# Two interleaved attention layers on one Trainium2 core: what the recurrent layer does at the border between two segments is reordered

## The chip, the cores and the metric

The kernel runs on one core of one Trainium2 chip. A core has five engines with an instruction queue each: PE (TensorE, matrix products; PEld are its weight loads), DVE (VectorE), ACT (ScalarE), POOL (GpSimd) and SP (SyncE, which here only issues transfers). They work side by side and wait for each other through semaphores. Sixteen DMA engines move data. TensorE writes to PSUM, eight banks of 2 KB per partition; everything else on the chip lies in SBUF.

The metric is the device time of one execution in microseconds (us), the median of several runs. The profile is of one execution of its own.

## The reference

The input x (1 x 2048 x 640) goes through four layers, A B A B, each added to its input after a layer norm. Layer B is a linear attention over all rows. Layer A is a recurrent attention with a memory:

```python
for s in range(n_seg):                       # 64 segments of 32 rows
    h = concat([mem, x[32 * s:32 * s + 32]]) # 8 memory rows + 32 rows, 640 columns
    q, k, v = h @ Wq, h @ Wk, h @ Wv         # 32 heads of 192
    p = softmax(mask(q k^T * scale))         # memory rows see all; others are causal
    o = (p v) @ Wo
    mem = o[:8]                              # the memory of the next segment
    outs.append(o[8:])
```

So the 64 segments of a layer form a chain: the first eight rows of one segment's output are inputs of the next segment's three projections.

## The kernel before

Everything the change touches is in the method A_chain, the chain of 64 segments of one layer A. The instructions are in an order written out by hand: each engine runs its own in the order in which the code issues them, with no scheduler between. Where an operation needs a result, a free buffer or a PSUM bank from another engine, it waits, and everything behind it on its engine's queue waits too.

**Rounds.** A segment has four rounds (n = 0 to 3) of eight heads. A round has the projections Q, K and V (project, L996 in the profile: 20 products each, of the transposed rows hT with 384 columns of weights), the scores (L1033 adds the mask, L1038 the six products), the exponential E (weigh, L1110), the product with the values (attend, L1049 into ps_o; L1056 into ps_t), the reciprocal of the sums rc (L1063), the scaling of the outputs osc (L1069 on ACT, L1071 on DVE), the transposition of osc to OT (turn, L1174 and L1181), and the output product with that round's part of Wo (wo_round, L1093), which adds up over the rounds in one PSUM bank, W. The rounds are interleaved: while the scores of round n are weighed, Q and K of round n+1 are projected.

**Copies.** Projections come out of PSUM on ACT as raw (to_raw, L1006), and DVE transposes them into QT and KT (to_rows, L1011 to L1016). V is copied by ACT for one half (L1025) and DVE for the other (L1027) into one of two tiles Vp.

**Rows that need no memory.** Of each segment's 32 rows, 24 go through the chain with the 8 memory rows. Keys, queries and values of the last 8 rows, the tails, were computed for all segments beforehand; POOL fetches them (kqb L967, Vp<-vb L979) and copies them into QT and KT (L972 to L975). The outputs of the tails collect in ps_t over two rounds and are weighed, transposed and stored for a later output product (keep_tail: reciprocal rct L1075, otr L1077 on ACT, otb L1079 on DVE; store_tail: L1083 on POOL).

**Weights.** Part of Wq, Wk, Wv and Wo stays in SBUF, and part takes turns: when round 0 has used a piece, SP loads the piece for round 3 of the same segment into its place (L680); after the output product of round 0 the same for Wo (L696). SP issues in the order Q, K, V, Wo.

**The border.** When W is complete, four partial sums lie in four partition groups of it. DVE transposes them into wt (L1244) in two pieces of the columns, 96 and 64, and adds the two halves into the first eight columns of hT (L1247). The first projections of the next segment start with the parts of hT that come first. Then keep_rows makes the 24 finished rows: ACT copies half of W to wh (L955), DVE adds the other half (L958), first for one half of the columns and then for the other. keep_tail follows. store_rows (L963, POOL) writes the rows after the next segment's Q0 and K0. A product with nothing to compute (keep_busy, L1099) and a weight load (fill, L1105) stand on PE between the segments. Most of hT for the next segment is transposed before that from rows fetched earlier (hx_transpose, L946).

**PSUM.** The eight banks are: two for Q and K, two for scores, one each for V, ps_o, ps_t and W.

Of the kernel before, what the change touches and what calls it, by code (L numbers as in the profile page):

```python
# [8 lines left out]
P = 128  # L9
BF16 = mybir.dt.bfloat16  # L10
F32 = mybir.dt.float32
ACT = mybir.ActivationFunctionType
ALU = mybir.AluOpType
# [104 lines left out]
class Kernel:  # L118
# [800 lines left out]
    def A_chain(self, xn_dram, at_dram, li, load_slot, piece, load_wo, late_wo, wo_mid, wo_end, low):  # L919
# [3 lines left out]
        with tc.tile_pool(name=f"A{li}_ch", reuse_waits="tile", bufs=1) as sp, \  # L923
# [27 lines left out]

            def keep_rows(W):
                tmp = [sp.tile([P, 160], F32, name=f"wh{a}", tag=tag) for a, tag in enumerate(("E", "rawk"))]
                for a in range(2):
                    last = nc.scalar.activation(out=tmp[a][64:P, :], in_=W[64:P, 160 * a:160 * a + 160], func=ACT.Copy)  # L955
                    for g in range(2):
                        c = 320 * a + 160 * g
                        nc.vector.tensor_tensor(out=orow[:, c:c + 160], in0=W[32 * g:32 * g + 32, 160 * a:160 * a + 160],  # L958
                                                in1=tmp[a][64 + 32 * g:96 + 32 * g, :], op=ALU.add)
                self.chain_end = [last]  # L960
# [57 lines left out]
            def v_rows(pv, n, which="ax"):  # L1018
                for x in range(2):
                    if "ax"[x] not in which:  # L1020
                        continue
                    o = self.two_heads(Vs[n % 2][0:64, 2 * VH * x:2 * VH * x + 2 * VH])
                    i = pv[64 * x:64 * x + 64, 0:384].rearrange("p (e f) -> p e f", e=2)
                    if x == 0:
                        nc.scalar.activation(out=o, in_=i, func=ACT.Copy)  # L1025
                    else:
                        nc.vector.tensor_copy(out=o, in_=i)  # L1027

            def scores():

                S = pop.tile([P, 512], F32, name="ps_s", tag="s", bufs=2)
                m = self.mk[0:80, :]
                nc.tensor.matmul(S[0:80, 0:320], lhsT=self.ident[0:80, 0:80], rhs=ap3(m, [list(m.ap[0]), [0, 4], [1, 80]]),  # L1033
                                 start=True, stop=False, skip_group_check=True)
                for x in range(2):
                    for i, q0, q1 in ((0, 0, 1), (1, 1, 3), (2, 3, 4)):
                        c0 = 160 * x + (80 if i == 2 else 0)
                        nc.tensor.matmul(S[0:80, c0:c0 + 80 * (q1 - q0)], lhsT=KT[:, 3 * x + i, :], rhs=QT[:, x, q0:q1, :],  # L1038
                                         start=False, stop=(x == 1 and i == 2), skip_group_check=True)
                return S  # L1040
# [32 lines left out]
            def keep_tail(tag):  # L1073
                rc = sp.tile([P, 1], F32, name="rct", tag="rct")
                nc.vector.reciprocal(out=rc[:], in_=pair[0][:, 192:193])  # L1075
                rows = sp.tile([P, 192], BF16, name="otr", tag=tag)
                nc.scalar.activation(out=rows[:], in_=pair[0][:, 0:192], func=ACT.Copy, scale=rc[:])  # L1077
                otb = sp.tile([P, 192], BF16, name="otb", tag="otb")
                self.chain_end.append(nc.vector.transpose(out=otb[:], in_=rows[:]))  # L1079
                return otb  # L1080
# [55 lines left out]
            for s in range(NSEG):  # L1136
                W = pop.tile([P, 512], F32, name="ps_w", tag="w")
# [22 lines left out]
                to_rows(q_or_k("K", 0), "K")  # L1160
                if s == 0:
                    late_wo(2)
                if s > 0:
                    store_rows(s - 1)
                pv = v_banks()
                project(hT, pv, "V", 0, s, range(KC))
                v_rows(pv, 0)
                OTs = []

                def turn(n, osc):  # L1170
# [9 lines left out]
                    for G, v in enumerate(OTs[n]):  # L1180
                        nc.vector.transpose(out=v, in_=osc[:, 192 * G:192 * G + 192].rearrange("p (c j) -> p c j", j=64))  # L1181
# [3 lines left out]
                for n in range(L):  # L1185
# [7 lines left out]
                    elif n == 2:  # L1193
                        wo_round(W, order[1], OTs[1], False, False, range(6))
                        self.chain_end = []
                        otb = keep_tail("rawk")
# [16 lines left out]
                    v_rows(pv, n + 1)  # L1213
# [11 lines left out]
                osc = sp.tile([P, 384], BF16, name="osc", tag="raw")  # L1225
                scaled(osc[:, 0:192], O, rc, 0, "s")
                scaled(osc[:, 192:384], O, rc, 1, "v")
                turn(L, osc)
# [11 lines left out]
                if s + 1 < NSEG:  # L1240
                    wt = [sp.tile([P, KC, 32], F32, name=f"wt{a}", tag=tag) for a, tag in enumerate(("raw", "rawk"))]
                    for b0, b1 in ((2, 5), (0, 2)):
                        for a in range(2):
                            nc.vector.transpose(out=wt[a][:, b0:b1, :],  # L1244
                                                in_=W[:, 160 * a:160 * a + 160].rearrange("p (j b) -> p b j", b=KC)[:, b0:b1, :])
                        for a in range(2):
                            nc.vector.tensor_tensor(out=hT[64 * a:64 * a + 64, b0:b1, 0:8], in0=wt[a][0:64, b0:b1, 0:8],  # L1247
                                                    in1=wt[a][64:P, b0:b1, 0:8], op=ALU.add)
                keep_rows(W)
                store_tail(keep_tail("OTh"), s, order[L])  # L1250
# [85 lines left out]
```

## Time and profile before

| | |
|---|---|
| time, median of 3 runs | 3744.9 us (3744.84 to 3748.18) |
| profiled execution, its own time | 3738.74 us |
| its span, first to last instruction | 3737.0 us |
| mean granted TensorE clock | 0.979 |
| PE busy | 3223.9 us (86%) |
| DVE busy | 2628.7 us (70%) |
| ACT busy | 1753.6 us (47%) |
| POOL busy | 1446.6 us (39%) |
| DMA | 927.76 MB, mean 248 GB/s |

A row of a timeline gives start, length, engine, line, operation, what is written and read, shapes and count; in brackets stand the idle time of the engine before it and what ended that. A row of the list of waits gives who waited for whom, the total in us, how often, and the longest. A stretch of time gives its length, the busy time of each engine with the number of instructions, the granted clock as a share of the full one, the busy share of the DMA engines and GB/s. The share can pass 1.0, since packets overlap. The two layers A take most of the span: 64 segments each, of some 22 us.

### The profile page before, as it was taken

How to read it: one execution, taken by the hardware profiler on the slowest of the kernel's cores; microseconds unless marked ns; L12 is line 12 of the kernel's file. 1: busy time of each engine (PE TensorE's matmuls, PEld its weight loads, DVE VectorE, ACT ScalarE, POOL GpSimd, SP SyncE). 2: the span in 40 equal slices, each digit the busy share in tenths (PEclk: the TensorE clock that was granted, in tenths of full speed). 3: DMA queues.
4: the chain of work that ended last, by engine and by line, in shares of the span. 5: the costliest groups of instructions: out<-in, count | busy, mean ns of one | idle time of the engine just before them, and what ended most of it. 6: DMA issues, size and time to landing. Idle time of an engine off the chain costs nothing.

```text
span 3737.0 us, 143258 instructions
## 1 busy us (share of the span) xinstructions
PE 3223.9 (86%) x58528; PEld 1965.6 (53%) x58834; DVE 2628.7 (70%) x7607; ACT 1753.6 (47%) x4225; POOL 1446.6 (39%) x3917
## 2 busy tenths in 40 slices
PE   9878888888888888889999788888888888888899
PEld 7644555555554555555467455555555555555553
DVE  5467777777777777756643677777777777777575
ACT  3244444444444444446533445444444444445463
POOL 3344444444444444431122344444444444444310
PEclk9999999999999999999999999999999999999999
DMA  8887777777777777770375878777777777788600
GB/s 321 322 284 260 269 279 276 272 265 272 279 278 260 273 267 278 267 248 12 124 270 206 282 264 280 277 268 266 263 276 273 273 269 259 267 281 280 237 4 29
DMA packets 444876, 927.76 MB, mean 248 GB/s; under 512 B 71722, under 2 KB 203450, under 8 KB 441146
## 3 DMA queue, kind: packets, MB, share of 16 engines
q1 hardware_dynamic: 382746, 821.50, 61.9%
q0 software_dynamic: 59552, 83.85, 7.1%
q10 hardware_dynamic: 1920, 13.24, 0.9%
q8 instruction: 461, 7.55, 0.8%
q14 instruction: 197, 1.61, 0.1%
HBM read 850.47 MB, written 75.69 MB: 248 GB/s over the span
## 4 chain that ended last, share of the span: by engine, by line
PE 42%; DVE 25%; DMA 10%; ACT 9%; issue 9%; POOL 3%; PEld 2%; ACTq 0%; SPq 0%; POOLq 0%; DVEq 0%
PE ps_qk L996 11%; PE ps_w L1093 8%; DMA Vp<-vb 7%; ACT osc L1069 4%; PE ps_v L996 4%; PE ps_pre L878 3%; PE ps_s L1038 3%; DVE Vp L958 3%; ACT otr L1077 2%; DVE KT L1011 2%; DVE QT L1014 2%; DVE otb L1079 2%; ACT wh L955 2%; PE kv L1291 2%; DVE Vp L1027 2%
## 5 line engine op out<-in xcount | busy, mean ns | idle before, releaser
L996 PE MATMUL ps_qk<-arena,hT 128*32 128x384 bf16 x20480 | 1051.7, 336 | 175.7 <-DVE hT L1247 96.0
L996 PEld LDWEIGHTS <-hT 128*32 128x32 bf16 x30720 | 784.2, 98 | 603.4 <-DVE hT L1247 159.4
L1006 ACT ACTIVATE raw<-ps_qk 128x384 bf16<-128x384 f32 x1024 | 489.2, 490 | 326.2 <-PE ps_qk L996 291.2
L996 PE MATMUL ps_v<-arena,hT 128*32 128x384 bf16 x10240 | 515.6, 328 | 9.6 <-DMA arena<-in_A_Wv_dram 9.6
L1093 PE MATMUL ps_w<-arena,OT 128*32 128x320 bf16 x9216 | 452.0, 303 | 8.1 <-DMA arena<-wo_rows 5.1
L1069 ACT ACTIVATE osc<-ps_o,rc 128x192 bf16<-128x192 f32 x896 | 335.3, 418 | 214.8 <-DVE rc L1063 214.1
L972 POOL COPY QT<-kqb 128x64 bf16<-128x64 bf16 x512 | 120.1, 235 | 644.8 <-PE ps_s L1038 585.4
L967 POOL DMA_DIRECT2D kqb<-kqb x512 | 290.5, 568 | 165.3 <-POOL KT L975 147.1
L1083 POOL DMA_DIRECT2D otb<-otb x256 | 143.8, 562 | 533.8 <-DVE otb L1079 506.9
L1014 DVE STREAM_TRANSPOSE QT<-raw 128x256 bf16<-128x256 bf16 x512 | 222.5, 434 | 177.3 <-PE ps_s L1038 157.3
L1110 ACT ACTIVATE E<-ps_s 80x320 bf16<-80x320 f32 x512 | 220.4, 431 | 268.5 <-PE ps_s L1038 267.8
L1011 DVE STREAM_TRANSPOSE KT<-raw 128x384 bf16<-128x384 bf16 x512 | 296.1, 578 | 54.0 <-ACT raw L1006 45.1
L955 ACT ACTIVATE wh<-ps_w 64x160 f32<-64x160 f32 x256 | 76.6, 299 | 507.7 <-PE ps_qk L996 366.0
L1027 DVE CAST Vp<-ps_v 64x384 bf16<-64x384 f32 x512 | 286.0, 559 | 27.4 <-ACT Vp L1025 11.5
L1038 PE MATMUL ps_s<-QT,KT 128*80 128x80 bf16 (+1 forms) x3072 | 233.8, 213 | 81.7 <-DVE KT L1011 48.5
L1093 PEld LDWEIGHTS <-OT 128*32 128x32 bf16 x9216 | 221.5, 96 | 143.1 <-DVE OT L1174 66.5
L979 POOL DMA_DIRECT2D Vp<-vb x512 | 258.7, 505 | 24.6 <-PE ps_t L1056 9.7
L1038 PEld LDWEIGHTS <-KT 128*80 128x80 bf16 x3072 | 198.2, 119 | 126.7 <-issue 112.9
L1093 PE MATMUL ps_w<-arena,KT 128*32 128x320 bf16 x3072 | 133.9, 310 | 143.2 <-DVE KT L1181 142.6
L1025 ACT ACTIVATE Vp<-ps_v 64x384 bf16<-64x384 f32 x512 | 246.6, 482 | 19.6 <-PE ps_v L996 19.5
L1049 PE MATMUL ps_o<-Vp,E 80*32 80x193 bf16 x4096 | 187.8, 249 | 39.7 <-DMA Vp<-vb 34.1
L878 PEld LDWEIGHTS <-arena 128*128 128x128 bf16 x1920 | 190.0, 99 | 43.5 <-issue 12.0
(155 smaller groups left out, 5053.7 us busy)
## 6 DMA issues: line engine op xcount, KB each, us to landing
arena<-wo_rows SPq DMA_DIRECT2D x804, 320.0 KB, 6.9
arena<-in_A_Wq_dram SPq DMA_DIRECT2D x427, 384.0 KB, 4.4
arena<-in_A_Wv_dram SPq DMA_DIRECT2D x427, 384.0 KB, 6.2
arena<-in_A_Wk_dram SPq DMA_DIRECT2D x768, 192.0 KB, 5.7
kqb<-kqb POOLq DMA_DIRECT2D x512, 48.0 KB, 4.9
arena<-in_A_Wk_dram SPq DMA_DIRECT2D x43, 384.0 KB, 7.8
vb<-arena POOLq DMA_DIRECT2D x128, 97.0 KB, 6.2
Vp<-vb POOLq DMA_DIRECT2D x512, 24.2 KB, 4.8
```

The costliest lines, as they stand in the source:

```text
L878: nc.tensor.matmul(ps[:, T * i:T * i + T], lhsT=w[b][:, P * c:P * c + P], rhs=xBT[:, b, :], start=(b == 0), stop=(b == KC - 1))
L967: nc.gpsimd.dma_start(out=kqb[:], in_=self.kqb_d[r, :, s, :])
L979: nc.gpsimd.dma_start(out=Vs[n % 2][64:80, :], in_=self.vb_d[s, r].rearrange("g t f -> (g t) f"))
L996: nc.tensor.matmul(o[32 * g:32 * g + 32, 0:384], lhsT=hT[:, b, :], rhs=rhs, start=(i == 0), stop=(i == KC - 1), tile_position=(0, 32 * g), ...
L1006: nc.scalar.activation(out=raw[:], in_=ps[:, 0:384], func=ACT.Copy)
L1011: nc.vector.transpose(out=KT[:, :, 0:64], in_=raw[:, :].rearrange("p (c j) -> p c j", j=64))
L1014: nc.vector.transpose(out=QT[:, :, 0:4:3, 0:64], in_=rv[:, :, 0:3:2, :])
L1025: nc.scalar.activation(out=o, in_=i, func=ACT.Copy)
L1027: nc.vector.tensor_copy(out=o, in_=i)
L1038: nc.tensor.matmul(S[0:80, c0:c0 + 80 * (q1 - q0)], lhsT=KT[:, 3 * x + i, :], rhs=QT[:, x, q0:q1, :], start=False, stop=(x == 1 and i == 2 ...
L1069: nc.scalar.activation(out=out, in_=i, func=ACT.Copy, scale=rc[:, G:G + 1])
L1093: nc.tensor.matmul(W[q:q + 32, 0:320], lhsT=OT[i // 6][:, i % 6 // 2, 32 * (i % 2):32 * (i % 2) + 32], rhs=rhs, start=(first and i < 2), s ...
```

## The change

- **Finished rows.** keep_rows and store_rows leave the border. They run in round 0 of the next segment, after turn(0) and ahead of the V copies of round 1. For that W gets two PSUM banks, and the scores one instead of two. Both ACT copies now come first, into one tile, and then the four adds.
- **Tails at the border.** keep_tail is split in three: the reciprocal stays at the end of the segment, otr comes after Q0 and K0 have been copied by ACT, otb and its store after the V copies of round 0.
- **Last outputs.** In the last round the first half of osc is scaled by DVE and the second by ACT, into two tiles; before, ACT had the first half and DVE the second, in one tile.
- **V copies.** Those of rounds 1 and 3 are both on ACT; those of rounds 0 and 2 stay on ACT and DVE.
- **wt.** The transposes and adds that make the memory columns of hT are no longer done in two pieces.

```diff
             def keep_rows(W):
-                tmp = [sp.tile([P, 160], F32, name=f"wh{a}", tag=tag) for a, tag in enumerate(("E", "rawk"))]
+                half = sp.tile([P, 160], F32, name="wh", tag="E")
                 for a in range(2):
-                    last = nc.scalar.activation(out=tmp[a][64:P, :], in_=W[64:P, 160 * a:160 * a + 160], func=ACT.Copy)
+                    nc.scalar.activation(out=half[64 * a:64 * a + 64, :], in_=W[64:P, 160 * a:160 * a + 160], func=ACT.Copy)
+                for a in range(2):
                     for g in range(2):
                         c = 320 * a + 160 * g
-                        nc.vector.tensor_tensor(out=orow[:, c:c + 160], in0=W[32 * g:32 * g + 32, 160 * a:160 * a + 160],
-                                                in1=tmp[a][64 + 32 * g:96 + 32 * g, :], op=ALU.add)
-                self.chain_end = [last]
+                        last = nc.vector.tensor_tensor(out=orow[:, c:c + 160], in0=W[32 * g:32 * g + 32, 160 * a:160 * a + 160],
+                                                       in1=half[64 * a + 32 * g:64 * a + 32 * g + 32, :], op=ALU.add)
+                self.chain_end.append(last)
...
-            def v_rows(pv, n, which="ax"):
+            def v_rows(pv, n, engines):
                 for x in range(2):
...
-                    if x == 0:
+                    if engines[x] == "s":
                         nc.scalar.activation(out=o, in_=i, func=ACT.Copy)
                     else:
                         nc.vector.tensor_copy(out=o, in_=i)
...
-                S = pop.tile([P, 512], F32, name="ps_s", tag="s", bufs=2)
+                S = pop.tile([P, 512], F32, name="ps_s", tag="s")
...
-            def keep_tail(tag):
+            def weigh_tail():
                 rc = sp.tile([P, 1], F32, name="rct", tag="rct")
                 nc.vector.reciprocal(out=rc[:], in_=pair[0][:, 192:193])
+                return rc
+
+            def tail_rows(rc, tag):
                 rows = sp.tile([P, 192], BF16, name="otr", tag=tag)
                 nc.scalar.activation(out=rows[:], in_=pair[0][:, 0:192], func=ACT.Copy, scale=rc[:])
+                return rows
+
+            def turn_tail(rows):
                 otb = sp.tile([P, 192], BF16, name="otb", tag="otb")
...
-                W = pop.tile([P, 512], F32, name="ps_w", tag="w")
+                W = pop.tile([P, 512], F32, name="ps_w", tag="w", bufs=2)
...
-                to_rows(q_or_k("K", 0), "K")
+                raw = q_or_k("K", 0)
+                if s > 0:
+                    rows = tail_rows(rct, "OTh")
+                to_rows(raw, "K")
                 if s == 0:
                     late_wo(2)
-                if s > 0:
-                    store_rows(s - 1)
                 pv = v_banks()
                 project(hT, pv, "V", 0, s, range(KC))
-                v_rows(pv, 0)
+                v_rows(pv, 0, "sv")
+                if s > 0:
+                    store_tail(turn_tail(rows), s - 1, rounds(s - 1)[L])
...
                     turn(n, osc)
-                    v_rows(pv, n + 1)
+                    if n == 0 and s > 0:
+                        keep_rows(W_done)
+                        store_rows(s - 1)
+                    v_rows(pv, n + 1, "sv" if n == 1 else "ss")
...
-                osc = sp.tile([P, 384], BF16, name="osc", tag="raw")
-                scaled(osc[:, 0:192], O, rc, 0, "s")
-                scaled(osc[:, 192:384], O, rc, 1, "v")
-                turn(L, osc)
+                oscs = [sp.tile([P, 192], BF16, name=f"osc{G}", tag=tag)[:] for G, tag in enumerate(("raw", "OTh"))]
+                for G in range(2):
+                    scaled(oscs[G], O, rc, G, "vs"[G])
+                turn(L, oscs)
...
-                    for b0, b1 in ((2, 5), (0, 2)):
-                        for a in range(2):
-                            nc.vector.transpose(out=wt[a][:, b0:b1, :],
-                                                in_=W[:, 160 * a:160 * a + 160].rearrange("p (j b) -> p b j", b=KC)[:, b0:b1, :])
-                        for a in range(2):
-                            nc.vector.tensor_tensor(out=hT[64 * a:64 * a + 64, b0:b1, 0:8], in0=wt[a][0:64, b0:b1, 0:8],
-                                                    in1=wt[a][64:P, b0:b1, 0:8], op=ALU.add)
-                keep_rows(W)
-                store_tail(keep_tail("OTh"), s, order[L])
+                    for a in range(2):
+                        nc.vector.transpose(out=wt[a][:], in_=W[:, 160 * a:160 * a + 160].rearrange("p (j b) -> p b j", b=KC))
+                    for a in range(2):
+                        nc.vector.tensor_tensor(out=hT[64 * a:64 * a + 64, :, 0:8], in0=wt[a][0:64, :, 0:8],
+                                                in1=wt[a][64:P, :, 0:8], op=ALU.add)
+                rct = weigh_tail()
+                W_done = W
+            store_tail(turn_tail(tail_rows(rct, "OTh")), NSEG - 1, order[L])
+            keep_rows(W_done)
             store_rows(NSEG - 1)
```

More of the change, by code (lines that the diff above doesn't have):

```diff
@@ L1016, in to_rows @@
                     nc.vector.transpose(out=QT[64:P, :, 2, 0:64], in_=rv[64:P, :, 1, :])
-            def v_rows(pv, n, which="ax"):
+            def v_rows(pv, n, engines):
                 for x in range(2):
-                    if "ax"[x] not in which:
-                        continue
                     o = self.two_heads(Vs[n % 2][0:64, 2 * VH * x:2 * VH * x + 2 * VH])
                     i = pv[64 * x:64 * x + 64, 0:384].rearrange("p (e f) -> p e f", e=2)
-                    if x == 0:
+                    if engines[x] == "s":
                         nc.scalar.activation(out=o, in_=i, func=ACT.Copy)
@@ L1071, in scaled @@
                     nc.vector.tensor_scalar(out=out, in0=i, scalar1=rc[:, G:G + 1], scalar2=None, op0=ALU.mult)
-            def keep_tail(tag):
+            def weigh_tail():
                 rc = sp.tile([P, 1], F32, name="rct", tag="rct")
                 nc.vector.reciprocal(out=rc[:], in_=pair[0][:, 192:193])
+                return rc
+            def tail_rows(rc, tag):
                 rows = sp.tile([P, 192], BF16, name="otr", tag=tag)
                 nc.scalar.activation(out=rows[:], in_=pair[0][:, 0:192], func=ACT.Copy, scale=rc[:])
+                return rows
+            def turn_tail(rows):
                 otb = sp.tile([P, 192], BF16, name="otb", tag="otb")
-                self.chain_end.append(nc.vector.transpose(out=otb[:], in_=rows[:]))
+                self.chain_end = [nc.vector.transpose(out=otb[:], in_=rows[:])]
                 return otb
@@ L1179, in turn @@
                         OTs.append([sp.tile([P, 3, 64], BF16, name="OT1", tag=tag)[:] for tag in ("rawk", "OTh")])
-                    for G, v in enumerate(OTs[n]):
-                        nc.vector.transpose(out=v, in_=osc[:, 192 * G:192 * G + 192].rearrange("p (c j) -> p c j", j=64))
+                    parts = osc if n == L else [osc[:, 192 * G:192 * G + 192] for G in range(2)]
+                    for v, part in zip(OTs[n], parts):
+                        nc.vector.transpose(out=v, in_=part.rearrange("p (c j) -> p c j", j=64))
                 if s == NSEG - 1:
@@ L1194, in A_chain @@
                         wo_round(W, order[1], OTs[1], False, False, range(6))
-                        self.chain_end = []
-                        otb = keep_tail("rawk")
+                        otb = turn_tail(tail_rows(weigh_tail(), "rawk"))
                     E = weigh()
```

## The prediction

> **What bounds the kernel now.** I read the page first, then who waited for whom, then one border between two segments in order of time, then that segment in stretches. The page's chain of work that ended last changes hands all the time:
>
> ```profile
> PE 42%; DVE 25%; DMA 10%; ACT 9%; issue 9%; POOL 3%; PEld 2%; ACTq 0%; SPq 0%; POOLq 0%; DVEq 0%
> ```
>
> TensorE is busy 86% of the span, so no engine's busy time is the bound; the waits at the border are. From the list of waits (us in total, times, longest):
>
> ```profile
> ACT otr L1077 <- DVE rct L1075: 145.9, 241, 0.9
> ...
> PE ps_w L1093 <- DVE KT L1181: 142.6, 128, 1.4
> ...
> ACT wh L955 <- DVE Vp L958: 91.7, 128, 0.7
> DVE osc L1071 <- ACT osc L1069: 70.3, 128, 0.6
> ...
> PE ps_qk L996 <- ACT raw L1006: 63.3, 106, 1.0
> ...
> PE ps_s L1038 <- DVE KT L1011: 48.5, 108, 0.5
> ...
> PE ps_o L1049 <- DMA Vp<-vb: 34.1, 47, 2.6
> ```
>
> The 128s are one per segment. I take the segment whose last output product ends at 660.25 (W below) as the example. In order of time, PE, ACT and DVE:
>
> ```profile
> 659.25 1.00 PE L1093 MATMUL ps_w<-arena,KT 128*32 128x320 bf16 x24 [1.37 <-DVE KT L1181]
> ...
> 661.23 0.67 PE L996 MATMUL ps_qk<-arena,hT 128*32 128x384 bf16 x12 [0.77 <-DVE hT L1247]
> ...
> 664.77 1.00 PE L996 MATMUL ps_qk<-arena,hT 128*32 128x384 bf16 x20 [0.59 <-ACT raw L1006]
> ...
> 666.48 0.45 PE L1038 MATMUL ps_s<-QT,KT 128*80 128x80 bf16 x6 [0.45 <-DVE KT L1011]
> ```
>
> ```profile
> 662.72 0.30 ACT L955 ACTIVATE wh<-ps_w 64x160 f32<-64x160 f32 x1 [0.72 <-DVE Vp L958]
> 663.92 0.42 ACT L1077 ACTIVATE otr<-ps_t,rct 128x192 bf16<-128x192 f32 x1 [0.90 <-DVE rct L1075]
> 664.24 0.86 ACT L1006 ACTIVATE raw<-ps_qk 128x384 bf16<-128x384 f32 x2
> ```
>
> ```profile
> 657.78 0.17 DVE L1063 RECIPROCAL rc<-ps_o 128x2 f32<-128x2 f32 x1
> 658.50 0.42 DVE L1071 TENSOR_SCALAR osc<-ps_o,rc 128x192 bf16<-128x192 f32 x1 [0.55 <-ACT osc L1069]
> ```
>
> Q0's product is done near 662.6, but ACT copies it out only at 664.24, behind two wh copies and otr, which wait for DVE's adds. So PE waits 0.59 for a free bank and the first scores 0.45 for KT.
>
> The stretches (PE, PEld, DVE, ACT, POOL busy; granted clock; DMA share; GB/s) show a second bound:
>
> ```profile
> 662.75:666.75 4.00, 2.96 (x63) 1.70 (x55) 3.09 (x9) 2.30 (x6) 1.09 (x2) 1.00 0.89 283
> 666.75:670.75 4.00, 3.99 (x102) 2.41 (x99) 3.00 (x8) 2.48 (x6) 1.91 (x6) 1.00 1.03 372
> ...
> 674.75:678.75 4.00, 4.00 (x93) 2.69 (x90) 3.15 (x9) 3.10 (x8) 2.85 (x9) 1.00 1.04 372
> ...
> 679.75:682.10 2.35, 1.67 (x39) 0.98 (x39) 1.73 (x6) 0.42 (x1) 0.94 (x2) 1.00 0.20 56
> ```
>
> From about W+2.5 to W+18.5 the DMA engines are full: the weights for the last round come in order (Q, K, V, wo), each freed by this segment's work. In the trace's landings the last wo piece arrives 20.49 after W (median; mean 20.52; 94 segments), and its round starts at W+20.84 at the earliest. The slack is a third of a microsecond.
>
> From one W to the next the trace has 21.84 at the shortest, 22.02 median, 22.23 mean, over 126 intervals. The profiled execution took 3738.7; the median of the runs, 3744.9, stands 6.2 above, which I keep. A difference under 0.2% (7 us) counts as no change.
>
> **The change part by part**, for one border.
>
> *V rows on ACT in rounds 1 and 3.* Two DVE casts (0.559 each) become two ACT copies (0.482 alone, about 0.42 more behind another). Before round 3 the first hT transposes, 0.73, stand behind the cast at 656.43, and rc behind both until 657.78, though attend ended at 657.39. Without the cast DVE is free at 657.16. On ACT the second copy pushes E from 656.33 to about 656.60, attend ends near 657.4, rc starts at 657.48: -0.30 (bounds 0 and -0.56, the whole cast).
>
> *Last outputs.* The two scalings read one PSUM bank and stay in order: the built program makes ACT wait for DVE now, where DVE waited for ACT. But DVE's own half no longer stands ahead of the first transpose. From the end of rc: scaling 0.42 and transpose 0.36 (with 0.05 between) let PE start at 0.90, before 1.30. The second half waits for ACT (0.50 to 0.92) and its transpose (to 1.33), so W comes at 1.98 instead of 2.30; the other two hT transposes, 0.74, then reach to 2.10 and the wt transposes start at 2.13, before 2.35. By wt: -0.22, with rc -0.52 (bounds -0.2 and -0.7).
>
> *Transposes of wt in one piece.* 96 columns take 0.262, 64 take 0.229; 160 are not in the trace. By the slope 0.33 (upper bound 0.49, the sum). Two of them 0.59, two adds 0.42, 0.09 of gaps: Q0 starts 1.12 after wt instead of 0.93, but runs its five groups of 0.164 through, where it waited for the second half until 1.75. Q0 is done at 1.92 instead of 2.08: -0.16 (bounds -0.16 and +0.2).
>
> *keep_rows and the tail leave the border.* ACT copies Q0 about 2.0 earlier, right behind its product. Then K0, V0 and Q1 follow each other on PE at 0.82 each; Q1 starts 1.64 after K0 instead of 2.39: -0.75. KT is ready 0.2 before the mask is in, so scores follow Q1 by 1.10, as in the other rounds, instead of 1.69: -0.59. The otb transpose, 0.38, now stands on DVE ahead of Q1's transposes and costs round 0 about 0.16, and POOL's store of it delays the QT copies, needed 4 us later.
>
> *keep_rows in round 0.* DVE: four adds, 1.30, in place of the cast and the 1.12 idle before L1014: 0.38 spare. ACT: two wh (0.57) and the second V copy (0.42) in place of idle 0.33 and 1.06: about 0.3 spare. If that cover went, every microsecond would come back in full. POOL: the row store (0.52) waits for the adds with QT's copies, kqb and the next Vp load queued behind it: 0.27 later. SP's order is unchanged. One scores bank instead of two: E ends 1.5 before the next mask; nothing.
>
> Sum on the engines: -0.52 - 0.16 - 0.75 - 0.59 + 0.16 = -1.86 per border, 234 us over 126.
>
> *What is late next: the loads.* Q0's first weights are freed at about W+1.53 instead of W+1.37, since all of hT comes at once; everything behind is a full DMA queue. So the last wo piece lands at 20.52 + 0.16 = 20.68, and its four products and their end (0.31) with 0.06 of signalling put the next W at 21.05, though the engines could be there at 19.9. Of 22.23 the floor leaves 1.18. V's last piece and the Vp load of round 3 (already 47 waits) also come late; mostly inside the same wait, 0.07 beyond it.
>
> *The clock.* Here row and rule part. Two neighbouring stretches of 3.41 us at one border, and one at another:
>
> ```profile
> 614.16:617.57 3.41, 1.60 (x41) 0.79 (x38) 2.65 (x11) 0.42 (x1) 1.59 (x3) 1.00 0.10 22
> 617.57:620.98 3.41, 3.41 (x44) 1.67 (x48) 2.41 (x10) 1.37 (x4) 0.00 (x0) 0.50 0.58 191
> 658.53:661.94 3.41, 1.88 (x37) 0.95 (x38) 3.13 (x13) 0.24 (x1) 0.63 (x2) 1.00 0.16 42
> ```
>
> PE busy 1.60 of 3.41 is followed by half the clock for the next 3.41; 1.88 is not. Over layer 1, of the stretches on this grid, the cut ones had 0.38 to 0.57 before them, the uncut at least 0.47. At present about 22% of the borders are cut, and intervals with a cut average 22.55. After the change PE trickles through the last wo pieces from W-2.1 to W, then waits 1.1 for hT: about 1.4 of 3.41 busy, for twice as many positions of the grid: 44% cut. Each loses up to 1.7 of PE work right at Q0, of which the loads' wait hides most: 0.45 left, 0.2 on the mean.
>
> By the Trainium skill (TensorE: Matmul & The Clock Gate, Part 1) the clock drops after an idle window of about 3.4 us; by that rule no border here would be cut, and the sum would lack this 0.2. The stretch at 614.16 was not idle and was cut, so the trace disagrees.
>
> Sum: 1.18 - 0.07 - 0.21 = 0.90 per border, 113 us over 126. 3744.9 - 113 = 3632.
>
> **The rivals.**
>
> *The clock is cut no more often than now.* 1.11 per border: 140 us, 3605. For: half the border's old waits on PE are gone. Against: the new wait is inside the output product.
>
> *The loads are no floor.* If the queue shortens with the engines' work, 1.86 stands: 234 us, 3511. For: a share over 1.0 only says that packets overlap. Against: the landings stay near W+20.5 in short and long intervals alike.
>
> *The change is hidden by loads before the last.* Vp and V loads, 5 to 6 us from issue to landing, were aimed at the old times; if they take 0.6 to 0.9 per border back, 0 to 0.3 remains: 3707 to 3745.
>
> *Slower: a second cut window.* If the cut lasted two windows (7 of the 28 cuts in the A layers did), 3.4 us of PE work would be lost at the border, 2.25 beyond the floor. From 49% of the borders (1.11/2.25) it eats the gain; at all of them the time is 3744.9 + 126 x 1.14 = 3889. Against: at half clock the same products fill the window (3.41 of 3.41 above).
>
> **How the numbers follow.** Forecast with the floor and more cuts 0.52 (3590 to 3690 with the bounds of wt, of rc and 0 to 0.45 of clock); no more cuts 0.15; no floor 0.10; hidden 0.12, of it 0.04 within 0.2%; second window 0.11. Faster 0.85, same 0.04, slower 0.11. The range 3545 to 3712 leaves out slower, most of hidden, and half of no floor.
>
> **What would show it.** Right: osc L1070 starts 0.03 behind rc; raw of Q0 comes right behind its product; the first scores at W+4.8 instead of W+6.2; PE ps_w waits for the DMA of wo_rows at most borders (now 5.7 us in all), intervals near 21.1; more stretches at 0.50. Wrong: intervals near 20 mean no floor; long waits on Vp or arena from V in rounds 2 and 3 mean hidden; scores of round 1 waiting for DVE's adds mean that round 0's cover is gone.

## The result and the profile after

The changed kernel takes 3722.4 us (median of 6 runs, 3709.5 to 3732.7) against 3746.6 before (6 runs, 3744.8 to 3749.6): a ratio of 0.9934, 95% interval 0.9913 to 0.9955. It is faster by 24 us; 113 were forecast, and the time lies 10 us above the top of the range. The profiled execution took 3717.45 with a span of 3715.7, 21 us under that of before; the decomposition below is of these two.

The engines' steps came out as the prediction lists them. One border whose clock was never cut, with W at 539.63 (the end of the last output product); first the timeline of TensorE (start, duration, what ran, then the idle time before it and who ended it):

```profile
537.82 0.97 PE L1098 MATMUL ps_w<-arena,KT 128*32 128x320 bf16 x20 [0.64 <-DVE KT L1190]
539.31 0.32 PE L1098 MATMUL ps_w<-arena,KT 128*32 128x320 bf16 x4 [0.53 <-DMA arena<-wo_rows]
...
540.77 1.81 PE L997 MATMUL ps_qk<-arena,hT 128*32 128x384 bf16 x40 [0.95 <-DVE hT L1256]
...
544.30 0.45 PE L1037 MATMUL ps_s<-QT,KT 128*80 128x80 bf16 x6
```

The same border on VectorE, and on ScalarE:

```profile
536.73 0.17 DVE L1062 RECIPROCAL rc<-ps_o 128x2 f32<-128x2 f32 x1 [0.88 <-PE ps_o L1048]
536.93 0.42 DVE L1070 TENSOR_SCALAR osc<-ps_o,rc 128x192 bf16<-128x192 f32 x1
537.38 0.89 DVE L1190 STREAM_TRANSPOSE KT<-osc 128x192 bf16<-128x192 bf16 x2
...
539.68 0.58 DVE L1254 STREAM_TRANSPOSE wt<-ps_w 128x160 f32<-128x160 f32 x2 [0.65 <-PE ps_w L1098]
540.29 0.43 DVE L1256 TENSOR_TENSOR hT<-wt 64x40 bf16<-64x40 f32 x2
```

```profile
541.87 0.49 ACT L1007 ACTIVATE raw<-ps_qk 128x384 bf16<-128x384 f32 x1 [4.01 <-PE ps_qk L997]
542.63 0.49 ACT L1007 ACTIVATE raw<-ps_qk 128x384 bf16<-128x384 f32 x1 [0.27 <-PE ps_qk L997]
543.02 0.41 ACT L1079 ACTIVATE otr<-ps_t,rct 128x192 bf16<-128x192 f32 x1
```

osc starts 0.03 behind rc, the last output product 0.92 behind it (0.90 forecast), the two wt transposes take 0.58 (0.59 forecast), Q0 starts at W+1.14, its raw copy follows its product, and the scores come at W+4.67 (4.8 forecast, 6.2 before). But the last four matmuls of the output product wait 0.53 for the last piece of Wo. That wait, 5.7 us in all before, is now there 90 times, at 67 of the borders; from the list of waits (us in total, times, longest):

```profile
PE ps_o L1048 <- DMA Vp<-vb: 82.9, 94, 3.0
PE ps_w L1098 <- DVE KT L1190: 79.3, 128, 0.7
...
PE ps_w L1098 <- DMA arena<-wo_rows: 51.6, 90, 3.0
```

The page's chain of work that ended last says the same: DMA had 10% of the span before and has 26% now, and two loads stand right behind Q's and K's products.

```profile
PE 34%; DMA 26%; issue 18%; DVE 9%; POOL 8%; ACT 3%; PEld 2%; SPq 0%; POOLq 0%; ACTq 0%; DVEq 0%
PE ps_qk L997 11%; DMA Vp<-vb 10%; DMA arena<-wo_rows 9%; PE ps_v L997 4%; DMA arena<-in_A_Wv_dram 4%; PE ps_w L1098 3%; PE ps_pre L878 2%; PE kv L1302 2%; POOL kqb L968 2%; DVE hT L946 1%; PE ps_o L1048 1%; PEld L878 1%; ACT osc L1068 1%; PE ps_s L1037 1%; DVE wt L1254 1%
```

Over the 126 intervals from W to W the mean is 21.97, before 22.23; 21.33 was forecast. The rest of the shortfall is at the two ends of an A layer, which the prediction did not price (below). For what follows I split the intervals by whether TensorE's clock was at half between W-2.5 and W+8 at the border that begins them (worked out from the traces' clock records and output products; us):

| kernel | cut: number, mean interval | not cut: mean (median) | first Wq load issued at W+ | last Wo piece lands at W+ |
|---|---|---|---|---|
| before | 25, 22.17 | 22.25 (22.02) | 1.39 | 20.52 |
| after | 45, 22.62 | 21.62 (21.50) | 1.60 | 21.00 |

After the change two things set the end. At the 81 borders without a cut it is mostly the last Wo piece: W follows its landing by less than 0.45 at 41 of the 50 where the landing is on record. At the 45 with a cut it does so at 7 of 44, though the piece lands no later there (20.94 on the mean, against 21.06). There the attention of round 3 ends last: its E is done at W+19.04 instead of 17.65, its product with the values waits for Vp at 39 of the 45 and starts at 19.79 instead of 18.15. One such segment, which began with a cut behind the W at 827.36 and whose last Wo piece landed at 848.27:

```profile
847.39 0.35 PE L1048 MATMUL ps_o<-Vp,E 80*32 80x193 bf16 x8 [1.26 <-DMA Vp<-vb]
...
848.88 1.50 PE L1098 MATMUL ps_w<-arena,KT 128*32 128x320 bf16 x24 [0.55 <-DVE KT L1190]
```

The last product waits here for its own input from DVE, not for Wo.

### The profile page after: what moved, and what is told of

The parts are those of the page before. It is cut to its first block, busy times and chain, and to the rows that moved or that the text cites. A ratio compares the mean times of both kernels' runs of the same rounds, so it can differ in the third digit from the quotient of the medians.

```text
span 3715.7 us, 143106 instructions
## 1 busy us (share of the span) xinstructions
PE 3252.8 (88%) x58528; PEld 1974.1 (53%) x58834; DVE 2428.5 (65%) x6847; ACT 1916.8 (52%) x4481; POOL 1448.0 (39%) x3917
## 3 DMA queue, kind: packets, MB, share of 16 engines
q14 instruction: 196, 1.61, 0.1%
## 4 chain that ended last, share of the span: by engine, by line
PE 34%; DMA 26%; issue 18%; DVE 9%; POOL 8%; ACT 3%; PEld 2%; SPq 0%; POOLq 0%; ACTq 0%; DVEq 0%
PE ps_qk L997 11%; DMA Vp<-vb 10%; DMA arena<-wo_rows 9%; PE ps_v L997 4%; DMA arena<-in_A_Wv_dram 4%; PE ps_w L1098 3%; PE ps_pre L878 2%; PE kv L1302 2%; POOL kqb L968 2%; DVE hT L946 1%; PE ps_o L1048 1%; PEld L878 1%; ACT osc L1068 1%; PE ps_s L1037 1%; DVE wt L1254 1%
## 5 line engine op out<-in xcount | busy, mean ns | idle before, releaser
L997 PE MATMUL ps_qk<-arena,hT 128*32 128x384 bf16 x20480 | 1062.9, 342 | 123.7 <-DVE hT L1256 117.3
L997 PEld LDWEIGHTS <-hT 128*32 128x32 bf16 x30720 | 806.5, 100 | 557.1 <-DVE hT L1256 116.2
L1007 ACT ACTIVATE raw<-ps_qk 128x384 bf16<-128x384 f32 x1024 | 502.1, 490 | 876.8 <-PE ps_qk L997 837.3
L997 PE MATMUL ps_v<-arena,hT 128*32 128x384 bf16 x10240 | 533.9, 334 | 19.8 <-DMA arena<-in_A_Wv_dram 19.6
L1024 ACT ACTIVATE Vp<-ps_v 64x384 bf16<-64x384 f32 x768 | 371.8, 484 | 42.4 <-PE ps_v L997 34.1
L1098 PE MATMUL ps_w<-arena,KT 128*32 128x320 bf16 x3072 | 173.1, 324 | 128.4 <-DVE KT L1190 79.3
L1048 PE MATMUL ps_o<-Vp,E 80*32 80x193 bf16 x4096 | 181.8, 249 | 93.6 <-DMA Vp<-vb 82.9
L1037 PEld LDWEIGHTS <-KT 128*80 128x80 bf16 x3072 | 209.5, 119 | 51.3 <-issue 31.7
L1062 DVE RECIPROCAL rc<-ps_o 128x2 f32<-128x2 f32 x512 | 87.1, 170 | 194.2 <-PE ps_o L1048 172.3
L946 DVE STREAM_TRANSPOSE hT<-Vp 32x160 bf16<-32x160 bf16 x512 | 181.7, 355 | 32.8 <-PE ps_v L997 12.7
```

The lines of the kernel that those rows point to most:

```text
L997: nc.tensor.matmul(o[32 * g:32 * g + 32, 0:384], lhsT=hT[:, b, :], rhs=rhs, start=(i == 0), stop=(i == KC - 1), tile_position=(0, 32 * g), ...
L1007: nc.scalar.activation(out=raw[:], in_=ps[:, 0:384], func=ACT.Copy)
L1098: nc.tensor.matmul(W[q:q + 32, 0:320], lhsT=OT[i // 6][:, i % 6 // 2, 32 * (i % 2):32 * (i % 2) + 32], rhs=rhs, start=(first and i < 2), s ...
```

## The experiments

### The loads as floor: no reload of the last round's Wo

From the changed kernel, and the same edit on the kernel before:

```diff
-                        if s < NSEG - 1:
-                            load_wo(order[L])
-                        else:
+                        if s == NSEG - 1:
                             tails = [self.fetch_tails(tb, low) for tb in range(2)]
```

> The changed kernel without the reload of the last round's Wo piece by piece (six loads of 320 KB a segment, 126 segments): the last round then multiplies by whatever lies in that buffer, so the output is not the reference's; every matmul stays. Theory 1 (the loads are the floor): the engines could have begun the last output product at W+19.9 and need about 0.6 from there, so uncut intervals fall from 21.48 to 20.2 to 20.6, the list of waits loses arena<-wo_rows, and the time falls by 130 to 185 us to 3540 to 3590. Theory 2 (no floor; the interval is long because of the clock and of other waits): uncut intervals stay within 0.3 of 21.48 and the time is 3680 to 3720.

> The kernel before with the same loads left out (output not the reference's either). Theory 1 (its engines' path is its bound and the loads end just inside it): the interval stays at 21.8 to 22.1, the time at 3715 to 3747. Rival (the loads slow the kernel by contention whatever its path, so leaving them out gains in both kernels alike): 3560 to 3610, as much as in the changed kernel.

Measured: the changed kernel 3498.5 us (2 runs, 3496.0 to 3500.9; ratio 0.9334, 0.9313 to 0.9355), the kernel before 3708.6 (2 runs; 0.9895, 0.9873 to 0.9917). The edit takes some 224 us from the one (3722.4, taken against other runs of the kernel before) and 40 from the other (3748.5, taken beside it). The median interval is 19.91 in the changed kernel and 21.85 in the other: with the load out of the way the change is worth 1.94 a border, where the prediction's sum on the engines had 1.86. (By the means, which hold the remaining cuts, 21.95 and 20.22, it is 1.73.) It also said that the engines could be at the next W at 19.9. Theory 1 stands, and by more than its own numbers: 3498 lies below its 3540 to 3590, since the uncut intervals, expected at 20.2 to 20.6, have a median of 19.91 and only 6 cuts are left in the two A layers (46 before the edit). The kernel before came out 6 us under its 3715: the loads took 0.28 a border (22.23 to 21.95) there too, which the third of a microsecond of slack had hidden from me.

In the list of waits of the changed kernel without the reload, the waits for Wo and for Vp are nearly gone (51.6 and 82.9 before the edit):

```profile
PE ps_w L1098 <- DMA arena<-wo_rows: 5.4, 5, 2.6
...
PE ps_o L1048 <- DMA Vp<-vb: 4.6, 9, 1.3
```

So the second wait is a child of the same queue, and the edit takes both away at once: the Vp load of round 3 is issued at W+12.65 and lands at 18.40 in the changed kernel (means of 126 borders), 5.7 us; without the Wo pieces it takes from 12.17 to 15.82, 3.6 us, for 24 KB. The Trainium skill (DMA: Bandwidth & Descriptors, Queues, rings and completion order) says that each DMA engine goes round between the queues that have work, a packet at a time; the longer way of a small load beside a full queue agrees with that, though no run here shows the turns themselves.

### The engines' terms by themselves

With the Wo reload left out as above, one part undone at a time: the transposes of wt in two pieces (the lines of before, the diff shown further down), and the V rows of rounds 1 and 3 on both engines.

```diff
-                    v_rows(pv, n + 1, "sv" if n == 1 else "ss")
+                    v_rows(pv, n + 1, "sv")
```

> The changed kernel without the reload of the last round's Wo (output not the reference's) and with the hidden state's transposes in two pieces again: the prediction's term for that part alone, with the loads out of the way. By the prediction (one piece saves the engines 0.16 a border): 126 x 0.16 = 20 us more than the 3498 of the kernel without the reload, 3518, median interval 20.07. Rival (two pieces are better for the engines too, which would explain why they gained 41.6 us with the loads in place): 3457 to 3490, median interval under 19.8.

> The changed kernel without the reload of the last round's Wo (output not the reference's) and with the V rows of rounds 1 and 3 split over ACT and DVE as before: the prediction's term of 0.30 alone. By the prediction: 126 x 0.30 = 38 us more than 3498, 3536, median interval 20.2 (bounds 0 and 0.56: 3498 to 3569). Rival (the first transposes of hT do not stand in the way of rc in the changed order): 3498, median interval 19.91.

Measured, against 3498.5 and a median interval of 19.91: wt in two pieces 3493.5 (2 runs, 3491.7 to 3495.3), median 20.07; V rows as before 3529.5 (2 runs, 3528.7 to 3530.3), median 20.18. The medians are those forecast, +0.16 and +0.27 (0.30 forecast). The V rows' 38 us came out as 31. The 20 us of the one-piece transposes did not come at all: the mean interval is 20.15 with two pieces and 20.22 with one, where no interval has a clock cut with two pieces and 6 have one with one. What this part saves on the common path it loses again in the clock. The other three terms of the sum were not tried alone.

### wt in two pieces, with the loads in place

```diff
-                    for a in range(2):
-                        nc.vector.transpose(out=wt[a][:], in_=W[:, 160 * a:160 * a + 160].rearrange("p (j b) -> p b j", b=KC))
...
+                    for b0, b1 in ((2, 5), (0, 2)):
+                        for a in range(2):
+                            nc.vector.transpose(out=wt[a][:, b0:b1, :],
+                                                in_=W[:, 160 * a:160 * a + 160].rearrange("p (j b) -> p b j", b=KC)[:, b0:b1, :])
...
```

> The changed kernel with the wt transposes and adds in two pieces of columns again, as before. Theory 1: Q0's first weights are used earlier, the first load is issued at W+1.37 instead of W+1.63, the last Wo piece lands 0.2 us earlier and with it every W: 25 us faster than after, 3697. Theory 2: Q0 is done 0.16 us later, 20 us slower, 3742.

Measured: 3680.8 (3669.3 to 3697.9; ratio 0.9829, 0.9806 to 0.9852), 41.6 us under the changed kernel. The direction of theory 1, and 16 us more than it gave. Q0 starts at W+0.98 again, the first Wq load is issued at 1.44 on the mean instead of 1.60, the last Wo piece lands at 20.79 instead of 21.00, the 0.2 of theory 1. Of the 33 us by which the 126 intervals of the two profiled executions differ, the tables give 14 to the intervals without a cut (0.11 each) and 20 to the cuts (45 x 1.00 against 37 x 0.68), so more than half is in the clock. Without the Wo reload, where hardly a border is cut, the same edit was worth 5 us. Cuts that lasted two or three windows fell from 20 to 8. Three neighbouring stretches of 3.41 us at such a border show why. The columns are length, then the busy time of PE, PEld, DVE, ACT and POOL, granted clock, DMA share, GB/s. The changed kernel:

```profile
845.93:849.34 3.41, 1.59 (x44) 0.78 (x36) 1.65 (x5) 0.68 (x2) 1.87 (x6) 1.00 0.28 94
849.34:852.75 3.41, 2.68 (x33) 1.13 (x34) 1.85 (x7) 0.00 (x0) 0.56 (x2) 0.50 0.13 31
852.76:856.17 3.41, 3.41 (x48) 1.73 (x44) 1.52 (x4) 1.29 (x3) 0.00 (x0) 0.50 0.86 293
```

The changed kernel with two pieces:

```profile
728.31:731.72 3.41, 1.41 (x38) 0.72 (x36) 1.63 (x5) 0.96 (x3) 1.92 (x6) 1.00 0.48 163
731.72:735.13 3.41, 2.83 (x35) 1.31 (x38) 2.47 (x11) 0.07 (x1) 0.52 (x1) 0.50 0.09 21
735.14:738.55 3.41, 3.41 (x81) 2.05 (x74) 2.30 (x7) 1.95 (x5) 0.00 (x0) 1.00 0.74 243
```

In both, a stretch at under half leads to a cut. Inside the cut TensorE is busy 2.68 of 3.41 in the one, and the cut stays; 2.83 in the other, and it is lifted. The difference is the later start of Q0 (W+1.15 against W+0.98 in these two). Over both A layers, windows at half clock after which the cut stayed were busy for 0.52 to 0.80 in the changed kernel and at most 0.76 with two pieces; those after which it was lifted for at least 0.78 and 0.77. Eight of the changed kernel's 21 that stayed lie at 0.79 or 0.80, right on that edge. It is no sharp edge: in the kernel before the cut once stayed after 0.84.

### The cuts of the clock: idle products

After the last output product the kernel runs one product that nothing reads, to keep TensorE busy. Here four of them, and in the changed kernel also one behind each of four pieces of that product:

```diff
-                wo_round(W, order[L], OTs[L], False, True)
                 idle = pqp.tile([P, 512], F32, name="ps_idle", tag="qk")
-                keep_busy(idle, 512)
+                for i in range(0, 12, 2):
+                    wo_round(W, order[L], OTs[L], False, True, range(i, i + 2))
+                    if 2 <= i < 10:
+                        keep_busy(idle, 512)
+                for _ in range(4):
+                    keep_busy(idle, 512)
```

> The changed kernel with idle products on PE: four of 512 columns (0.21 us each) instead of one between the end of W and the next Q0, and one more behind each of the pieces 2 to 5 of the last output product, where PE waits for Wo. Theory 1 (the loads set the interval, and the cut clock adds to it): intervals between two W with the clock at one half fall from 55 of 126 to under 20, the mean interval from 21.97 to about 21.5, the time by some 55 us, to about 3667. Theory 2 (the engines' own path did not become shorter as reckoned): PE has no time to give away, each border gets 0.8 to 1.6 us longer, the time is above 3800.

> The kernel before with four idle products instead of one between W and Q0, the control. The wait there is 0.77 us, so three more fit nearly. Theory 1: fewer stretches at half clock (31 of 126 intervals now), but these cost only 0.4 us each there, so at most 10 us faster, 3735 to 3747. Theory 2: the same. If the idle products themselves were worth something apart from the clock, it would show here.

Measured: the changed kernel 3709.3 (3704.2 to 3714.7; 0.9901, 0.9884 to 0.9918); the kernel before 3755.3 (3752.4 to 3763.2; 1.0026, 1.0015 to 1.0037), a little slower rather than level. Cut borders fell from 45 to 15 in the changed kernel, yet it gained 13 us, neither theory's number; the intervals of the two ratios, 0.9901 and 0.9934, just touch. With 15 cut borders left the mean interval is 21.86: the last Wo piece still lands at 20.96, and the idle products themselves now lengthen the uncut intervals from 21.62 to 21.84. By the tables the cuts cost 45 us before and 2 now, and the longer uncut intervals took 28 of that back, two thirds.

### The ends of the layers

The prediction priced 126 borders and nothing else. In the changed kernel the first products of layer B come 9.5 us after the last W of layer A (3.9 before). TensorE there, before:

```profile
1616.05 1.00 PE L1093 MATMUL ps_w<-arena,KT 128*32 128x320 bf16 x24 [1.02 <-DVE KT L1181]
...
1620.97 0.22 PE L1292 MATMUL ps_post<-arena 128*128 128x128 bf16 x1 [3.71 <-DVE arena L89]
```

After, and ScalarE's copies of the finished rows in that trace:

```profile
1600.58 0.32 PE L1098 MATMUL ps_w<-arena,KT 128*32 128x320 bf16 x4 [0.57 <-DMA arena<-wo_rows]
...
1610.41 0.27 PE L1303 MATMUL ps_post<-arena 128*128 128x128 bf16 x1 [9.32 <-DVE Vp L959]
```

```profile
1604.94 3.04 ACT L91 ACTIVATE arena<-arena 128x768 bf16<-128x768 bf16 x4 [5.96 <-DMA arena<-otb]
1607.88 0.40 ACT L1079 ACTIVATE otr<-ps_t,rct 128x192 bf16<-128x192 f32 x1
1608.31 0.61 ACT L955 ACTIVATE wh<-ps_w 64x160 f32<-64x160 f32 x2
```

Layer B's first accumulator takes the PSUM bank of the last W, and now waits until its rows are read out, which stand on ScalarE behind 3 us of other copies that wait for a load. From the last W of layer 1 to the first of layer 2 it is 472.8 us (467.1 before), from the last W of layer 2 to the end 258.3 (252.4): 11 to 12 us together. Two single banks taken in turn let the last segment's W lie elsewhere:

```diff
-                W = pop.tile([P, 512], F32, name="ps_w", tag="w", bufs=2)
+                W = pop.tile([P, 512], F32, name="ps_w", tag=f"w{s % 2}")
```

> The changed kernel with the two PSUM banks of W allocated under two names, so that the last segment of a layer A has its W in another bank than the one that layer B's first products use. Seen in the trace of after: these products start 9.5 us behind the last W instead of 3.9, right after the last add of keep_rows. If that bank is the cause, both layer ends get 5.6 us shorter: 11 us faster than after, about 3711. If it is the order of the work at the end (tail first, rows later), nothing changes.

Measured: 3714.3 (3697.3 to 3722.4; 0.9901, 0.9879 to 0.9924), 8 us less, where 11 were expected. The runs of the two kernels overlap, so the time alone would leave it unclear; the traces show it. Layer B's products start 4.9 after W, and the two stretches are 469.8 and 253.9, 7 us shorter together. The two later profiles with two names have 468.7 to 470.4 and 251.8 to 252.9; the eight of the changed kernel and its versions with one name 471.3 to 475.4 and 257.3 to 260.9.

```profile
1603.04 0.32 PE L1098 MATMUL ps_w<-arena,KT 128*32 128x320 bf16 x4 [0.80 <-DMA arena<-wo_rows]
...
1608.23 0.31 PE L1303 MATMUL ps_post<-arena 128*128 128x128 bf16 x1 [4.68 <-DVE arena L89]
```

### Parts undone or alone

V rows as before, the rest of the change kept (the diff shown above):

> The changed kernel with the V rows of rounds 1 and 3 split over ACT and DVE again, as before the change: one part undone. Theory 1 (the loads end last, the attention's end before the last product is hidden under them): rc comes 0.3 later at each border, the last product starts later, but the interval stays, 3716 to 3729. Rival (the 0.3 lies on the path that sets the interval): 126 x 0.3 = 38 us more, about 3760.

Measured: 3721.0 (3714.3 to 3730.6; 0.9929, 0.9912 to 0.9945), the time of the changed kernel to 2 us. The 31 us that this part was worth without the reload of Wo are worth nothing under the floor, as theory 1 has it.

Only the finished rows and the tails moved; on top of the two pieces, V rows as before and the last outputs as before:

```diff
-                    v_rows(pv, n + 1, "sv" if n == 1 else "ss")
+                    v_rows(pv, n + 1, "sv")
...
-                oscs = [sp.tile([P, 192], BF16, name=f"osc{G}", tag=tag)[:] for G, tag in enumerate(("raw", "OTh"))]
-                for G in range(2):
-                    scaled(oscs[G], O, rc, G, "vs"[G])
-                turn(L, oscs)
+                osc = sp.tile([P, 384], BF16, name="osc", tag="raw")
+                scaled(osc[:, 0:192], O, rc, 0, "s")
+                scaled(osc[:, 192:384], O, rc, 1, "v")
+                turn(L, [osc[:, 0:192], osc[:, 192:384]])
```

> One part alone: the changed kernel with V rows, last outputs and the hidden state's transposes as before, so that only the finished rows (two banks) and the tails move. Theory 1 (loads are the floor, so only what lets the loads start early counts): as much as with the two pieces alone undone, 3674 to 3690. Rival (the parts add up on the engines' path, 0.30 and 0.22 a border lost): 3681 + 126 x 0.52 = 3746.

Measured: 3732.0 (12 runs, 3711.7 to 3752.9; 0.9958, 0.9940 to 0.9976). The time is 42 us above theory 1's range and 14 below the rival's 3746. The last Wo piece lands earlier than in any other version with it (20.64), and the time is worse all the same. Two things are seen in the trace. First, another load sets the end. At uncut borders round 3's attend starts at W+18.40, 0.89 after its E is done, for want of Vp; from there the outputs of before need 1.92 to the first matmul of the last product and 1.00 to its end, which makes 21.32, while Wo, at 20.57 there, would allow 20.94 (0.37 behind it). With the V rows and outputs of the change it is 18.35 + 1.50 + 1.10 = 20.95, against 21.13 by Wo. Second, 66 borders are cut instead of 37. By the table below the first is 0.20 x 126 = 25 us on uncut intervals, the second about 29 x 0.68 = 20 us of cuts. The counts are of one execution each, and the two-name version below, whose segments run the same code as the two-piece one, had 54; but the mean granted clock of all runs goes the same way, 0.946 to 0.958 here and 0.960 to 0.971 with two pieces. So the earlier V rows, which were worth nothing above, are worth some 50 us together with the outputs when the loads start early. The outputs were not tried alone, nor why the cuts come so much more often.

### Together

Two pieces and the two bank names, without and with the idle products:

> The changed kernel with the hidden state's transposes in two pieces as before and the output product's two banks under two names. If the gains of the two single edits add up (41.6 and 8 us below the changed kernel): 3669 to 3678. Rival (the gain of the two pieces was mostly a chance of where the clock's windows fell): 3690 to 3710.

> The two-piece, two-name version with eight idle products per border (one behind each of four pieces of the last product, four after it in place of one) against the clock cuts. Theory 1 (cuts cost what they cost in the changed kernel, where the same products took 13 us off): 3658 to 3664. Rival (with the loads as floor the cuts are hidden, and the idle products stand in TensorE's way): 3674 to 3690.

Measured: 3674.1 (3666.2 to 3687.7; ratio 0.9800, 0.9783 to 0.9817), the sum of the single gains within 2 us, and the best version here. The gain of the two pieces came a second time, so it was no chance. With the idle products 3712.4 (3707.6 to 3718.7; 0.9909, 0.9894 to 0.9924): 38 us worse, beyond the rival's range. They cut the cut borders from 54 to 19 and lengthen the uncut intervals from 21.43 to 22.04 on the mean, for the four between the pieces stand ahead of the end of W: from the first matmul of the last output product to W the shortest border now takes 1.85, without them 1.05.

| kernel | cut: number, mean interval | not cut: mean (median) | first Wq load issued at W+ | last Wo piece lands at W+ |
|---|---|---|---|---|
| before, with idle products | 12, 22.37 | 22.40 (22.11) | 1.43 | 20.60 |
| after, with idle products | 15, 22.00 | 21.84 (21.61) | 1.55 | 20.96 |
| after, two bank names | 51, 22.68 | 21.64 (21.47) | 1.61 | 21.01 |
| after, V rows as before | 54, 22.51 | 21.60 (21.50) | 1.61 | 20.92 |
| after, wt in two pieces | 37, 22.19 | 21.51 (21.25) | 1.44 | 20.79 |
| rows and tails alone | 66, 22.39 | 21.71 (21.37) | 1.44 | 20.64 |
| two pieces, two names | 54, 22.33 | 21.43 (21.24) | 1.45 | 20.76 |
| the same with idle products | 19, 21.95 | 22.04 (21.78) | 1.39 | 20.73 |
| after, no Wo reload | 8, 21.35 | 20.14 (19.91) | 1.63 | none |
| before, no Wo reload | 24, 21.96 | 21.95 (21.85) | 1.39 | none |

## Why the prediction was wrong

The sign and the mechanism were right: the engines gained what was worked out (1.86 forecast, 1.94 measured without the load, by the median), and the loads kept most of it. The size was not: 113 us were forecast, 21 came between the two profiled executions, and 92 are to be accounted for. 81 of them are 126 times the 0.64 between the forecast mean interval of 21.33 and 21.97.

- **The floor by loads, 21.05.** This term was mis-sized. The step "the last wo piece lands at 20.52 + 0.16 = 20.68" moved the whole chain by the later first issue. In the uncut intervals the first issue was 1.57 (1.53 forecast), but from there to the last landing it took 19.49 instead of 19.14, and that landing at 21.06 is 0.38 above the forecast. From landing to W it took 0.56 on the mean instead of 0.37, since at 9 of 50 borders something else ended it. Together 21.62 in place of 21.05: 0.57 x 126 = 72 us, less the 0.07 (9 us) that I had allowed for V and Vp. The chain got longer by less in the version with V rows and outputs as before (from 1.37 to 20.57 in uncut intervals, 19.20) and by 0.2 with two pieces alone undone. Small loads of the engines, now further ahead, get between the Wo pieces: from the first issue to the last landing SP's queue moved 5.51 MB in both kernels, the other queues 0.482 MB instead of 0.445, at 307 GB/s instead of 311 (means of 49 and 74 uncut intervals). At that rate the 0.037 MB more are 0.12 us, a third of the 0.35; why the rest moved more slowly stays open.
- **Transposes of wt in one piece, -0.16.** Right for the engines (median 20.07 against 19.91). But the floor that the same text set up pays for a later first issue, so this part was a loss as soon as the floor ruled: undoing it gave 41.6 us, by the floor and by the clock. The prediction had both numbers of the floor, and took the part as given instead of asking what each part is worth under the floor.
- **The clock, 44% of the borders at 0.45.** The intervals with a cut in them were 55 of 126, the 44% forecast, and 45 were cut at their start. That the share is met so closely is luck: the version with two bank names, whose segments run the same code, had 60 of 126. A border with a cut cost 1.00 (22.62 against 21.62), not 0.45: 45 x 1.00 / 126 = 0.36 instead of 0.20, 20 us. The step that failed is that the loads' wait hides most of the loss. The start of round 3's attend came 1.64 later at the cut borders (19.79 against 18.15; its E 1.39 later), where up to 1.7 was forecast to be lost, and with 1.49 to the last product and 1.10 to its end W could come at 22.38 at the earliest, well behind the last Wo piece: the floor hid 0.64 of the 1.64. The rival of a second cut window was argued away with a stretch at half clock that was busy for 3.41 of 3.41; 20 of the changed kernel's 45 cut borders had cuts that lasted two windows or more, for the window that holds the new, later start of Q0 is often busy for 0.80 or less. But these 20 average 22.72 and the other 25 average 22.54, so most of the miss lies in the first window.
- **The layers' ends.** Not priced: 11 to 12 us. Two banks also decide which bank is free for what comes after the loop, and the rows are read out only 7.4 us behind W there, as late as in the loop (7.3 behind the W at 539.63).
- **Hidden by loads before the last.** Its place showed (waits for Vp 34.1 to 82.9 us), its time, 3707 to 3745, is where the kernel came out; but at the uncut borders it stands behind Wo in the changed kernel: attend of round 3 starts at 18.15, and with 1.49 to the last product and 1.10 to its end W could come at 20.74. At the cut borders the wait for Vp is part of what ends last, and with the last outputs of before it sets the end at uncut borders too. So this rival was right in part; how much of the shortfall would go if Vp came in time was not tried.
- **Slower, by a second window at the border.** It priced such a border at 2.25 beyond the floor and needed 49% of them; 20 of 126 had one and cost 1.10 (22.72 against 21.62).

Two readings of the kernel before were a little off and change none of this: two of its intervals, 21.50 and 21.65, are below the shortest that the prediction names, and in these the last product started at W+20.50 and 20.65, not at 20.84 at the earliest.

By the Trainium skill (TensorE: Matmul & The Clock Gate, Part 1) half the clock follows an idle window of about 3.4 us. The trace disagrees here as it did before: the changed kernel's cuts followed windows in which TensorE was busy for 0.32 to 0.56 of the time, and all of its 697 other windows at full clock, from the first W of a layer A to the last, had at least 0.45.

## What to carry to other kernels

When a transfer chain ends within half a microsecond of the engines' path, price every part of a change twice, once on the engines and once by what it does to the first transfer of that chain: a part that starts the chain later can be a loss although it saves engine time. Test the floor with the transfer left out before tuning what lies above it; here that one run told 224 us from 24. And where a loop hands its last buffer to the stage behind it, look at that hand-over by itself.

## What the runs showed of the hardware

- At half clock the cut of TensorE has an edge of its own. Windows of 3.41 us at half clock that were busy for up to 0.80 kept the cut in the changed kernel, those from 0.78 on lifted it, while at full clock windows above 0.56 were not followed by a cut. Over the A layers of all 14 traces both happened between 0.76 and 0.85 at half clock, and the busiest window at full clock that a cut followed had 0.60. A start 0.17 later (0.05 of a window) can decide between one window and two.
- Kernels with many cut borders spread more: with the rows alone moved, 66 cut borders in the profile, 12 runs lay between 3711.7 and 3752.9, 1.1%, and the longest had the lowest mean granted clock (0.946, against 0.958 for the shortest). The kernel before, 25 cut borders, had 17 runs within 0.4% on the same chip. That nearness to the edges makes the spread fits this and is not shown.
- A product that nothing reads is not free even where TensorE waits: four between the pieces of the last output product made the shortest way from its first matmul to W 1.85 instead of 1.10 in the changed kernel. In the best version the eight idle products of a border cost more than the cuts that they prevented.
